# Issuing the attention stage's input loads from GpSimd's DMA ring instead of SyncE's

## The chip, the cores and the metric

The kernel runs on one core of a Trainium2 chip. The metric is the device time of one execution in microseconds (us). A core has five engines, each of which runs its own instruction stream in order: TensorE (PE, with its weight loads shown as PEld), VectorE (DVE), ScalarE (ACT), GpSimd (POOL) and SyncE (SP). They are kept in step by semaphores. Data moves between device memory and the on-chip memory by DMA: an engine issues a transfer, and the transfer tells of its landing through a semaphore.

## The reference

The program is a recurrent attention over 4 x 8 heads, 768 steps and 40 dimensions, followed by a two-layer MLP over 3072 tokens.

```python
# attention, for each of 32 heads; state is 40 x 40
for t in range(S):
    y[:, :, t] = np.einsum('bhd,bhde->bhe', rt, state)
    Sa = np.einsum('bhde,bhe->bhd', state, at)
    state_decay = state * wt[:, :, None, :] - np.einsum('bhd,bhe->bhde', Sa, bt)
    state = state_decay + np.einsum('bhd,bhe->bhde', vt, kt)
# MLP, d_model 320, d_ff 2048
h = x @ w_in
sp = np.maximum(h, 0.0) + np.log1p(np.exp(-np.abs(h)))
out = (h * erf(sp)) @ w_out
```

`r, k, v, w, a, b` come in float32; the MLP's weights come in float64 and are turned into float32 on the chip.

## The kernel before

The 768 steps are cut into blocks of 128 (`L`) and these into chunks of 32 (`C`). The 32 heads are worked on in two groups of 16 (`NG` = 2, eight pairs each), one after the other, so there are 12 stages of four chunks, 48 chunks in all. Within a chunk the recurrence becomes matrix products: `prep` makes running products of the decay `w` for a block, `aphase` scales `k`, `b` and `a` with them and builds the chunk's small matrices, `tphase` inverts a block's triangular matrices, and `chain` carries the state through the chunk. `load_x`, `mm1`, `unit` and `post` are the MLP for tokens whose attention is done; it runs beside the attention of later stages.

The order is not left to the engines. Every operation is entered with `Plan.add` (name, engine, function, what it reads and writes), and `Plan.schedule` then returns an order written out by hand in the file: `ORDER` is a list of operation numbers, `ENGINES` a string with one letter for each operation (P for PE, A for ACT, V for DVE, G for POOL, S for SP). With these two of the right length, no planner runs. -1 and lower in `ORDER` are filler matmuls (`warm`, L579). Each engine gets its operations in this order, and waits where a buffer or an input isn't ready.

All 907 DMAs of the kernel are entered through one helper, `dma`, and issued by SP (L576 in the profile, whatever the transfer). Those of the attention are:

- the input loads: `w` (12, 420 KB each, into `Pr`, in `prep`), `kba` (48, 416 KB, into `bk`; three of the first stage go into other tiles that are free then), `zv` (48, 80 KB, into `Zm`), `vx` (96, 40 KB, into `Vu`), `rt` (48, 104 KB, into `Rt`), `rv` (48, 416 KB, into `vt`);
- transfers of results, on which the attention's own chain runs: `zs` (`Zs<-Ab`), `AD`, `Ti`, `Ap`, `TD`, `tb` (through device memory, to change the layout) and `zu` (`Vu<-Us`).

Besides these there are the MLP weights (`wd`), the attention's result (`xw`, `xd<-Pr`), its way back as the MLP's input (`xr`), and the output (`out`).

How many buffers a load has decides how early it can be issued: `Pr` has three, `bk`, `vt`, `Rt` and `Vu` two, `Zm` one. The previous content of a buffer is read last by: `bk` the products at L677 and the transposes at L695, `Zm` the products at L785 (Z), `Rt` and `Vu` the products at L841 and L845 (MY), `vt` the products at L830 (PQ).

POOL does 120 operations of its own in this order, above all 27 products `nd` (L1039) and 27 `l` (L1051) of the MLP's activation, 19 `bk` (L672) and 10 `ab` (L667) of the attention, and 20 `xl` (L990), the low part of the MLP's input. DVE does the other operations of these kinds. After `nd` comes DVE's `r` (L1040), after `l` DVE's `h` (L1052); `nd` has one buffer.

Of the kernel before, what the change touches and what calls it, by code (L numbers as in the profile page):

```python
# [200 lines left out]
)  # L201
ENGINES = (
    "SSSVVGVGVGAAAVVGAGVVVAASAVVVVSVSSVPVVSSPVSGSSVPVVSSPASVSSGPVVSSPASVSSVPVVSSPASSSSAAVVVVVVVVVVVVVVVVVVVVVVVVVVVVSSSSVPPPPVPPPPVSVVAAAGAGSVVAA"
    "AVAVSVVAAAGAVSVVAAAVAVSVVAAAVAVSVVAAAVAVSVVAAAVAVSVVAAAGAVSVVAAAGAAVAGSVVAAAGAAVAGSVVAAAVSVVAAAVSVVAAAGSVVAAAVSVVAAAGSVVAAAVSVVAAAVSVVAAAVSV"
    "VAAAGSVVAAAVSAVVAVSVSSVPVVSSPASVSSVPVVSSPVSVSSVPVVSSPASVSSGPVVSSPASSSSSAAPAPAAVAVPVPVPVPVVSSSSSAAPVPAAAVVPAPAPVPVVSSSSSAAPAPAAAAAPAPVPVPVVSS"
    "SSSAAPAPAAAAVPVPVPVPVVSSSSSSSSAAVVVVVVVVVVVVVVVVVVVVVVVVVVVVSSSSVPPPPVPPPPVSAGSVGSSVVPPVAPPVAPPAAPPVAAAAAAAAAAAAAAAVVVVVVVVAAAAAPPAAPPAAVVPP"
    "PPPPAAGVPPPPPPAAVVPPPPVVPPPPSAVVAVSVSSGPVVSSPASGSSGPVVSSPASVSSGPVVSSPASVSSGPVVSSPASSSSSVVAPAPASSSSPVPAPVPVVSSSSSAAPAPASSSSPVPVPVPVVSSSSSVVPV"
    "PASSSSPAPVPVPVVSSSSSAAPAPASSSSPAPAPVPVVSSSSSSSSAAVVVVVVVVVVVVVVVVVVVVVVVVVVVVSSSSVPPPPVPPPPVSVGSVVSSAVAAAAAAAAAAAAAAVVGVVVGVAAAAAPPAAPPAAVVP"
    "PPPPPAAVVPPPPPPAAGVPPPPVVPPPPASASAAAAAAAAAAAAAAGVVVGVVVAAAAAPPAAPPVAGVPPPPPPAAVVPPPPPPAAVVPPPPGVPPPPSAVVVVSVSSVPVVSSPASGSSVPVVSSPASVSSVPVVSS"
    "PASVSSVPVVSSPASSSSSVAAPVPASSSSPVPVPVPVVSSSSSAAPAPASSSSPAPAPVPVVSSSSSAAPAPASSSSPAPAPVPVVSSSSSAVPVPVSSSSPVPAPVPVVSSSSSSSSAAVVVVVVVVVVVVVVVVVVV"  # L210
    "VVVVVVVVVSSSSVPPPPVPPPPVSVGSVVSSAGAAAAAAAAAAAAAAVVGVVVVVAAAAAPPAAPPAAGVPPPPPPAAVVPPPPPPAAVVPPPPVVPPPPASASAAAAAAAAAAAAAAGVVVVVVVAAAAAPPAAPPAA"
    "VVPPPPPPAAVVPPPPPPAAVVPPPPVVPPPPSAVVVVSVSSVPVVSSPVSGSSVPVVSSPASVSSVPVVSSPASVSSVPVVSSPASSSSSVAAPVPVSSSSPAPAPVPVVSSSSSVVPAPASSSSPAPAPVPVVSSSSS"
    "VAPAPASSSSPAPAPVPVVSSSSSAAPAPASSSSPAPAPVPVVSSSSSSSSAAVVVVVVVVVVVVVVVVVVVVVVVVVVVVSSSSVPPPPVPPPPVSVGSAVSSAVAAAAAAAAAAAAAAVVGVVVVVAAAAAPPAAPPA"
    "AGVPPPPPPAAVVPPPPPPAAVVPPPPVVPPPPASASAAAAAAAAAAAAAAVVGVVVVVAAAAAPPAAPPAAVVPPPPPPVAVVPPPPPPAAGVPPPPVVPPPPSAVVAVSVSSVPVVSSPASVSSGPVVSSPASVSSVP"
    "VVSSPASVSSGPVVSSPASSSSSVAAPAPASSSSPAPVPVPVVSSSSSAVPAPVSSSSPVPVPVPVVSSSSSAAPAPASSSSPAPAPVPVVSSSSSAVPAPVSSSSPVPAPVPVVSSSSSSSSAAVVVVVVVVVVVVVVV"
    "VVVVVVVVVVVVVSSSSVPPPPVPPPPVSAGSAGSSVGAAAAAAAAAAAAAAVVGVVVGVAAAAAPPAAPPAAVVPPPPPPAAGVPPPPPPAAVVPPPPVVPPPPASASAAAAAAAAAAAAAAVVVVVVVVAAAAAPPAA"
    "PPAAVVPPPPPPAAVVPPPPPPAAVVPPPPVVPPPPSAVVVVSVSSGPVVSSPVSGSSGPVVSSPASVSSVPVVSSPASVSSGPVVSSPASSSSSVAAPAPVSSSSPVPVPVPVVSSSSSVAPAPVSSSSPAPAPVPVVS"
    "SSSSVAPAPASSSSPAPAPVPVVSSSSSAAPAPASSSSPAPVPVPVVSSSSSSSSAAVVVVVVVVVVVVVVVVVVVVVVVVVVVVSSSSVPPPPVPPPPVSAGSAGSSVVAAAAAAAAAAAAAAVVGVVVVVAAAAAPPA"
    "APPAAVVPPPPPPAAGVPPPPPPAAVVPPPPVVPPPPASASAAAAAAAAAAAAAAGVVVVVVVAAAAAPPVAPPAAVVPPPPPPVAVVPPPPPPAAVVPPPPVVPPPPSAVVVVSVSSGPVVSSPASGSSGPVVSSPVSV"
    "SSGPVVSSPASVSSVPVVSSPASSSSSVVAPVPVSSSSPVPAPVPVVSSSSSAAPAPASSSSPVPAPVPVVSSSSSVAPAPASSSSPAPAPVPVVSSSSSAVPAPASSSSPAPAPVPVVSSSSSSSSAAVVVVVVVVVVV"  # L220
    "VVVVVVVVVVVVVVVVVSSSSVPPPPVPPPPVSAGSVVSSVVAAAAAAAAAAAAAAVVVVVVVVAAAAAPPAAPPAAGVPPPPPPAAGVPPPPPPAAVVPPPPGVPPPPASASAAAAAAAAAAAAAAVVVVVVVVAAAAA"
    "PPAAPPAAGVPPPPPPAAGVPPPPPPVAGVPPPPGVPPPPSAVVAVSVSSVPVVSSPVSVSSGPVVSSPASVSSVPVVSSPASVSSVPVVSSPVSSSSSVAAPVPASSSSPAPVPVPVVSSSSSAAPAPASSSSPVPAPV"
    "PVVSSSSSAAPAPASSSSPAPAPVPVVSSSSSVAPAPASSSSPAPVPVPVVSSSSSSSSAAVVVVVVVVVVVVVVVVVVVVVVVVVVVVSSSSVPPPPVPPPPVSVVSAGSSAVAAAAAAAAAAAAAAGVGVVVVVAAAA"
    "APPAAPPAAVVPPPPPPAAVVPPPPPPAAVVPPPPGVPPPPASASAAAAAAAAAAAAAAVVGVGVVVAAAAAPPVAPPVAGVPPPPPPAAVVPPPPPPAAGVPPPPGVPPPPSAVVAVSVSSVPVVSSPASGSSGPVVSS"
    "PASVSSVPVVSSPVSGSSVPVVSSPASSSSSVAAPVPVSSSSPAPAPVPVVSSSSSAVPVPASSSSPVPVPVPVVSSSSSAAPAPASSSSPAPAPVPVVSSSSSAAPAPASSSSPAPAPVPVVSSSSSSSSAAVVVVVVV"
    "VVVVVVVVVVVVVVVVVVVVVSSSSVPPPPVPPPPVSVGSAVSSVVAAAAAAAAAAAAAAGVVVVVVVAAAAAPPVAPPAAVVPPPPPPAAVVPPPPPPAAVVPPPPVVPPPPVSASAAAAAAAAAAAAAAVVGVVVGVA"
    "AAAAPPVAPPAAVVPPPPPPAAVVPPPPPPAAGVPPPPVVPPPPSAVVVVSVSSVPVVSSPASVSSVPVVSSPASVSSVPVVSSPVSGSSVPVVSSPASSSSSVVAPAPVSSSSPAPAPVPVVSSSSSAVPVPASSSSPV"
    "PVPVPVVSSSSSAAPAPASSSSPAPAPVPVVSSSSSAAPAPASSSSPAPAPVPVVSSSSSSSSAAVVVVVVVVVVVVVVVVVVVVVVVVVVVVSSSSVPPPPVPPPPVSAGSVGSSVGAAAAAAAAAAAAAAGVGVVVGV"
    "AAAAAPPAAPPAAVVPPPPPPAAVVPPPPPPAAVVPPPPVVPPPPASASAAAAAAAAAAAAAAVVGVVVVVAAAAAPPAAPPAAVVPPPPPPAAVVPPPPPPVAGVPPPPGVPPPPSAVVAVSVSSVPVVSSPVSGSSGP"
    "VVSSPASVSSGPVVSSPASVSSGPVVSSPASSSSSGAVPAPVSSSSPVPAPVPVVSSSSSAAPAPASSSSPVPAPVPVVSSSSSAAPAPASSSSPVPAPVPVVSSSSSAAPAPASSSSPVPVPVPVVSSSSSSSSAAVVV"  # L230
    "VVVVVVVVVVVVVVVVVVVVVVVVVSSSSVPPPPVPPPPVSAVSAGSSAGAAAAAAAAAAAAAAVVVVVVGVAAAAAPPVAPPAAGVPPPPPPVAVVPPPPPPVAVVPPPPGVPPPPASASAAAAAAAAAAAAAAGVGVG"
    "VVVAAAAAPPVAPPAAVVPPPPPPAAVVPPPPPPAAVVPPPPGVPPPPSSSSSVAVPVPASSSSPVPAPVPVVSSSSSVVPAPVSSSSPAPAPVPVVSSSSSAVPAPASSSSPVPVPVPVVSSSSSVVPVPASSSSPVPA"
    "PVPVVSSSSVPVVSVVSVVSSVGAAAAAAAAAAAAAAVVVVVVVVAAAAAPPAAPPAAVVPPPPPPVAVVPPPPPPAAVVPPPPVVPPPPVSASAAAAAAAAAAAAAAVVVVVVVVAAAAAPPVAPPAAVVPPPPPPAAV"
    "VPPPPPPVAVVPPPPGVPPPPAAAAAAAAAAAAAAVVVVVVVVAAAAAVVPPPPVVPPPPVVPPPPVVPPPPASAS"
)
# [259 lines left out]
class Net:  # L495
# [77 lines left out]
            self.eng(e).tensor_copy(o, i)  # L573

    def dma(self, name, o, i, rd=(), wr=(), pr=0):
        self.P.add(name, "SP", lambda e: self.nc.sync.dma_start(o(), i()), rd, wr, pr, ISSUE.get(name, 0.41))  # L576
# [618 lines left out]
```

## Time and profile before

| | |
|---|---|
| median of 3 runs | 859.44 us (858.28 to 864.45) |
| the profiled execution | 857.22 us, its span 855.2 us |
| granted TensorE clock, mean | 0.97 |
| DMA | 185585 packets, 107.58 MB, mean 126 GB/s |
| POOL | 17% busy, 124 instructions |

The profiled execution is 0.26% under the median of the three runs. The time of a kernel lies some 2 us above its span. A row of the profile names the line, the engine, the operation and the tiles it writes and reads (`out<-in`); all DMA issues have line L576, the helper's, so they are told apart by their tiles. `SPq` is SP's queue. Idle time is given with what ended it: `<-DMA x` is a transfer that landed, `<-PE y` an operation that finished.

### The profile page before, as it was taken

The numbers are of one execution on the slowest core, as the hardware profiler recorded it, in microseconds if no ns is written. First come the engines' busy times: TensorE is split into PE (matmuls) and PEld (weight loads), VectorE is DVE, ScalarE is ACT, GpSimd is POOL, SyncE is SP. The second block draws the span as 40 slices with busy tenths as digits, with TensorE's granted clock in tenths as the row PEclk, the third lists the DMA queues.
The fourth block names the chain that finished last, engine by engine and source line by source line (L and its number), as shares of the span: only waits on it lengthen the run. The fifth ranks groups of instructions, "written<-read, shape, count | busy, mean of one in ns | idle before, by whom it ended". The sixth has DMA issues, their size and how long they took to land.

```text
span 855.2 us, 32264 instructions
## 1 busy us (share of the span) xinstructions
PE 741.9 (87%) x13794; PEld 572.6 (67%) x13794; DVE 626.0 (73%) x1331; ACT 563.6 (66%) x1055; POOL 145.3 (17%) x124
## 2 busy tenths in 40 slices
...
GB/s 213 216 155 156 172 157 119 134 135 142 135 169 115 145 139 123 138 121 143 160 122 118 139 130 115 158 109 146 141 112 128 126 112 92 123 39 66 36 16 19
DMA packets 185585, 107.58 MB, mean 126 GB/s; under 512 B 134268, under 2 KB 167804, under 8 KB 185436
## 3 DMA queue, kind: packets, MB, share of 16 engines
q1 hardware_dynamic: 185436, 105.46, 51.8%
...
q14 instruction: 39, 0.32, 0.1%
...
## 4 chain that ended last, share of the span: by engine, by line
PE 43%; DMA 21%; DVE 14%; SPq 8%; ACT 6%; issue 6%; POOL 1%; DVEq 0%; ACTq 0%; POOLq 0%
PE po L1061 15%; PE ph L1006 10%; SPq L576 8%; DMA Zs<-Ab 3%; PE pA L740 3%; DMA Ti<-AD 3%; PE ph L579 3%; DMA Tb<-TD 2%; PE my L841 2%; PE pQ L830 2%; PE pA L677 2%; DMA bk<-in_kba_e 2%; DMA AD<-Zs 2%; DVE h L1052 2%; PE my L794 2%
## 5 line engine op out<-in xcount | busy, mean ns | idle before, releaser
L1061 PE MATMUL po<-wo,h 128*128 128x320 f32 x768 | 255.1, 459 | 6.1 <-DVE h L1052 5.8
L1061 PEld LDWEIGHTS po<-wo,h 128*128 128x128 f32 x768 | 135.7, 195 | 51.4 <-DVE h L1052 8.7
L1014 ACT ACTIVATE l<-l 128x512 f32<-128x512 f32 x192 | 112.0, 625 | 18.2 <-DVE nd L1039 14.4
L1006 PE MATMUL ph<-xh,wih 128*128 128x256 f32 x384 | 96.1, 332 | 3.4 <-ACT h L571 3.4
L1006 PE MATMUL ph<-xh,wil 128*128 128x256 f32 x384 | 78.0, 285 | 0.0
L1006 PE MATMUL ph<-xl,wih 128*128 128x256 f32 x384 | 77.7, 284 | 0.0
L1052 DVE SCALAR_TENSOR_TENSOR h<-l,h 128x512 f32<-128x512 f32 x96 | 70.3, 739 | 3.0 <-POOL l L1051 2.1
L1040 DVE SCALAR_TENSOR_TENSOR r<-nd,r 128x512 f32<-128x512 f32 x96 | 68.1, 709 | 5.9 <-POOL nd L1039 4.8
L1039 POOL TENSOR_TENSOR nd<-l,r 128x512 f32<-128x512 f32 x27 | 35.7, 1321 | 206.9 <-DVE r L1040 120.4
L1006 PEld LDWEIGHTS ph<-xh,wih 128*128 128x128 f32 x384 | 61.3, 194 | 10.2 <-ACT h L571 4.3
L571 ACT COPY Zm<-MT 40x320 f32<-40x320 f32 x71 | 32.4, 457 | 50.5 <-DVE MT L848 45.6
L579 PE MATMUL ph<-d 104*128 104x512 bf16 x257 | 65.7, 407 | 0.0
L1051 POOL TENSOR_TENSOR l<-l,r 128x512 f32<-128x512 f32 x27 | 38.2, 1419 | 158.6 <-ACT l L1014 85.8
L1006 PEld LDWEIGHTS ph<-xh,wil 128*128 128x128 f32 x384 | 60.6, 194 | 3.9 <-issue 3.9
L1014 ACT ACTIVATE l<-h 128x512 f32<-128x512 f32 x96 | 57.2, 628 | 7.2 <-DVE h L573 6.0
L1006 PEld LDWEIGHTS ph<-xl,wih 128*128 128x128 f32 x384 | 60.2, 192 | 0.0
L1039 DVE TENSOR_TENSOR nd<-l,r 128x512 f32<-128x512 f32 x69 | 49.7, 721 | 11.6 <-ACT r L1014 9.5
L1006 PE MATMUL ph<-xl,wir 128*128 128x256 f32 x192 | 54.9, 286 | 3.8 <-issue 3.7
L841 PE MATMUL my<-Vu,sg 64*40 64x72 f32 x1536 | 48.5, 233 | 8.7 <-DVE h L1052 3.1
L1014 ACT ACTIVATE r<-r 128x512 f32<-128x512 f32 x96 | 55.2, 624 | 0.4
L1014 ACT ACTIVATE r<-l 128x512 f32<-128x512 f32 x96 | 54.2, 619 | 1.5 <-DVE l L1051 1.4
L1006 PE MATMUL ph<-xh,wir 128*128 128x256 f32 x192 | 54.8, 285 | 0.0
...
## 6 DMA issues: line engine op xcount, KB each, us to landing
vt<-in_rv_e SPq DMA_DIRECT2D x48, 416.0 KB
bk<-in_kba_e SPq DMA_DIRECT2D x45, 416.0 KB
...
```

The costliest lines, as they stand in the source:

```text
L571: self.nc.scalar.copy(o, i)
L576: self.P.add(name, "SP", lambda e: self.nc.sync.dma_start(o(), i()), rd, wr, pr, ISSUE.get(name, 0.41))
L579: self.nc.tensor.matmul((self.ph[1], self.pQ)[x], self.d1[:, :128], self.d1[:, :512], start=True, stop=True)
L740: nc.tensor.matmul(pw[js, i], l[js, i], r[js, i], start=True, stop=True)
L841: nc.tensor.matmul(my[h * 64:h * 64 + 40, x, j], sg[xs, j, h], vu[xs, j // 2 * 2 + h, j % 2], start=True, stop=False)
L1006: nc.tensor.matmul(ph[:, j * 256:j * 256 + 256], a[:k, fs], b[:k], start=(m == 0), stop=(m == 7))
L1014: self.P.add(name, "ACT", lambda e: nc.scalar.activation(out=o, in_=i, **kw), rd, wr + ["act"], pr, 0.62)
L1039: P.add("nd", [("DVE", 0.69), ("POOL", 1.28)], lambda e, r=r, l=l, nd=nd: s.eng(e).tensor_tensor(out=nd, in0=l, in1=r, op=ALU.mult), [("l" ...
L1040: P.add("rho", "DVE", lambda e, r=r, nd=nd: nc.vector.scalar_tensor_tensor(out=r, in0=nd, scalar=2 * C4, in1=r, op0=ALU.add, op1=ALU.mult) ...
L1051: P.add("E", [("POOL", 1.28), ("DVE", 0.69)], lambda e: s.eng(e).tensor_tensor(out=l, in0=l, in1=r, op=ALU.mult), [("r", ir)], [("l", il)] ...
L1052: P.add("G", "DVE", lambda e: nc.vector.scalar_tensor_tensor(out=h, in0=l, scalar=-1.0, in1=h, op0=ALU.add, op1=ALU.mult), [("l", il)], [( ...
L1061: nc.tensor.matmul(po, h[:, bs], s.wo[:, f], start=(f == 0), stop=(f == 15))
```

## The change

Six names of loads are put in a tuple `BULK`. `dma` enters a load of these names for POOL and issues it there; every other DMA stays with SP. In `ENGINES` the 300 letters of these loads turn from S to G, so that the list fits. `ORDER` is untouched: the loads keep their places among all operations, and so come into POOL's stream between the products that stand around them in `ORDER`, while SP's stream has 607 DMAs instead of 907.

```diff
@@ -200,36 +200,36 @@
 ENGINES = (
-    "SSSVVGVGVGAAAVVGAGVVVAASAVVVVSVSSVPVVSSPVSGSSVPVVSSPASVSSGPVVSSPASVSSVPVVSSPASSSSAAVVVVVVVVVVVVVVVVVVVVVVVVVVVVSSSSVPPPPVPPPPVSVVAAAGAGSVVAA"
...
+    "SSSVVGVGVGAAAVVGAGVVVAAGAVVVVGVSSVPVVSSPVGGSSVPVVSSPAGVSSGPVVSSPAGVSSVPVVSSPASSSSAAVVVVVVVVVVVVVVVVVVVVVVVVVVVVSSSSVPPPPVPPPPVSVVAAAGAGSVVAA"
...
@@ -253,6 +253,7 @@
 FREE = ("Am", "PQm", "MT", "Ym", "zt", "zmu", "us", "vtu", "ysM", "bTc", "ob", "hc", "Wm", "Tb", "zgb", "zcb")
+BULK = ("kba", "rt", "zv", "rv", "vx", "w")
...
@@ -573,7 +574,7 @@
     def dma(self, name, o, i, rd=(), wr=(), pr=0):
-        self.P.add(name, "SP", lambda e: self.nc.sync.dma_start(o(), i()), rd, wr, pr, ISSUE.get(name, 0.41))
+        self.P.add(name, "POOL" if name in BULK else "SP", lambda e: self.eng(e).dma_start(o(), i()), rd, wr, pr, ISSUE.get(name, 0.41))
```

`self.eng(e)` is `nc.gpsimd` for POOL and `nc.sync` for SP.

More of the change, by code (lines that the diff above doesn't have):

```diff
@@ L202 @@
 ENGINES = (
-    "SSSVVGVGVGAAAVVGAGVVVAASAVVVVSVSSVPVVSSPVSGSSVPVVSSPASVSSGPVVSSPASVSSVPVVSSPASSSSAAVVVVVVVVVVVVVVVVVVVVVVVVVVVVSSSSVPPPPVPPPPVSVVAAAGAGSVVAA"
+    "SSSVVGVGVGAAAVVGAGVVVAAGAVVVVGVSSVPVVSSPVGGSSVPVVSSPAGVSSGPVVSSPAGVSSVPVVSSPASSSSAAVVVVVVVVVVVVVVVVVVVVVVVVVVVVSSSSVPPPPVPPPPVSVVAAAGAGSVVAA"
     "AVAVSVVAAAGAVSVVAAAVAVSVVAAAVAVSVVAAAVAVSVVAAAVAVSVVAAAGAVSVVAAAGAAVAGSVVAAAGAAVAGSVVAAAVSVVAAAVSVVAAAGSVVAAAVSVVAAAGSVVAAAVSVVAAAVSVVAAAVSV"
-    "VAAAGSVVAAAVSAVVAVSVSSVPVVSSPASVSSVPVVSSPVSVSSVPVVSSPASVSSGPVVSSPASSSSSAAPAPAAVAVPVPVPVPVVSSSSSAAPVPAAAVVPAPAPVPVVSSSSSAAPAPAAAAAPAPVPVPVVSS"
@@ L206 @@
[L206 to L209, printed above, removed]
@@ L210 @@
-    "PASVSSVPVVSSPASSSSSVAAPVPASSSSPVPVPVPVVSSSSSAAPAPASSSSPAPAPVPVVSSSSSAAPAPASSSSPAPAPVPVVSSSSSAVPVPVSSSSPVPAPVPVVSSSSSSSSAAVVVVVVVVVVVVVVVVVVV"
+    "VAAAGSVVAAAVGAVVAVGVSSVPVVSSPAGVSSVPVVSSPVGVSSVPVVSSPAGVSSGPVVSSPAGGGGGAAPAPAAVAVPVPVPVPVVGGGGGAAPVPAAAVVPAPAPVPVVGGGGGAAPAPAAAAAPAPVPVPVVGG"
+    "GGGAAPAPAAAAVPVPVPVPVVSSSSSSSSAAVVVVVVVVVVVVVVVVVVVVVVVVVVVVSSSSVPPPPVPPPPVSAGSVGSSVVPPVAPPVAPPAAPPVAAAAAAAAAAAAAAAVVVVVVVVAAAAAPPAAPPAAVVPP"
+    "PPPPAAGVPPPPPPAAVVPPPPVVPPPPGAVVAVGVSSGPVVSSPAGGSSGPVVSSPAGVSSGPVVSSPAGVSSGPVVSSPAGGGGGVVAPAPASSSSPVPAPVPVVGGGGGAAPAPASSSSPVPVPVPVVGGGGGVVPV"
@@ L211 @@
+    "PASSSSPAPVPVPVVGGGGGAAPAPASSSSPAPAPVPVVSSSSSSSSAAVVVVVVVVVVVVVVVVVVVVVVVVVVVVSSSSVPPPPVPPPPVSVGSVVSSAVAAAAAAAAAAAAAAVVGVVVGVAAAAAPPAAPPAAVVP"
+    "PPPPPAAVVPPPPPPAAGVPPPPVVPPPPASASAAAAAAAAAAAAAAGVVVGVVVAAAAAPPAAPPVAGVPPPPPPAAVVPPPPPPAAVVPPPPGVPPPPGAVVVVGVSSVPVVSSPAGGSSVPVVSSPAGVSSVPVVSS"
+    "PAGVSSVPVVSSPAGGGGGVAAPVPASSSSPVPVPVPVVGGGGGAAPAPASSSSPAPAPVPVVGGGGGAAPAPASSSSPAPAPVPVVGGGGGAVPVPVSSSSPVPAPVPVVSSSSSSSSAAVVVVVVVVVVVVVVVVVVV"
     "VVVVVVVVVSSSSVPPPPVPPPPVSVGSVVSSAGAAAAAAAAAAAAAAVVGVVVVVAAAAAPPAAPPAAGVPPPPPPAAVVPPPPPPAAVVPPPPVVPPPPASASAAAAAAAAAAAAAAGVVVVVVVAAAAAPPAAPPAA"
-    "VVPPPPPPAAVVPPPPPPAAVVPPPPVVPPPPSAVVVVSVSSVPVVSSPVSGSSVPVVSSPASVSSVPVVSSPASVSSVPVVSSPASSSSSVAAPVPVSSSSPAPAPVPVVSSSSSVVPAPASSSSPAPAPVPVVSSSSS"
@@ L213 @@
-    "VAPAPASSSSPAPAPVPVVSSSSSAAPAPASSSSPAPAPVPVVSSSSSSSSAAVVVVVVVVVVVVVVVVVVVVVVVVVVVVSSSSVPPPPVPPPPVSVGSAVSSAVAAAAAAAAAAAAAAVVGVVVVVAAAAAPPAAPPA"
-    "AGVPPPPPPAAVVPPPPPPAAVVPPPPVVPPPPASASAAAAAAAAAAAAAAVVGVVVVVAAAAAPPAAPPAAVVPPPPPPVAVVPPPPPPAAGVPPPPVVPPPPSAVVAVSVSSVPVVSSPASVSSGPVVSSPASVSSVP"
-    "VVSSPASVSSGPVVSSPASSSSSVAAPAPASSSSPAPVPVPVVSSSSSAVPAPVSSSSPVPVPVPVVSSSSSAAPAPASSSSPAPAPVPVVSSSSSAVPAPVSSSSPVPAPVPVVSSSSSSSSAAVVVVVVVVVVVVVVV"
+    "VVPPPPPPAAVVPPPPPPAAVVPPPPVVPPPPGAVVVVGVSSVPVVSSPVGGSSVPVVSSPAGVSSVPVVSSPAGVSSVPVVSSPAGGGGGVAAPVPVSSSSPAPAPVPVVGGGGGVVPAPASSSSPAPAPVPVVGGGGG"
@@ L216 @@
+    "VAPAPASSSSPAPAPVPVVGGGGGAAPAPASSSSPAPAPVPVVSSSSSSSSAAVVVVVVVVVVVVVVVVVVVVVVVVVVVVSSSSVPPPPVPPPPVSVGSAVSSAVAAAAAAAAAAAAAAVVGVVVVVAAAAAPPAAPPA"
+    "AGVPPPPPPAAVVPPPPPPAAVVPPPPVVPPPPASASAAAAAAAAAAAAAAVVGVVVVVAAAAAPPAAPPAAVVPPPPPPVAVVPPPPPPAAGVPPPPVVPPPPGAVVAVGVSSVPVVSSPAGVSSGPVVSSPAGVSSVP"
+    "VVSSPAGVSSGPVVSSPAGGGGGVAAPAPASSSSPAPVPVPVVGGGGGAVPAPVSSSSPVPVPVPVVGGGGGAAPAPASSSSPAPAPVPVVGGGGGAVPAPVSSSSPVPAPVPVVSSSSSSSSAAVVVVVVVVVVVVVVV"
     "VVVVVVVVVVVVVSSSSVPPPPVPPPPVSAGSAGSSVGAAAAAAAAAAAAAAVVGVVVGVAAAAAPPAAPPAAVVPPPPPPAAGVPPPPPPAAVVPPPPVVPPPPASASAAAAAAAAAAAAAAVVVVVVVVAAAAAPPAA"
-    "PPAAVVPPPPPPAAVVPPPPPPAAVVPPPPVVPPPPSAVVVVSVSSGPVVSSPVSGSSGPVVSSPASVSSVPVVSSPASVSSGPVVSSPASSSSSVAAPAPVSSSSPVPVPVPVVSSSSSVAPAPVSSSSPAPAPVPVVS"
@@ L218 @@
-    "SSSSVAPAPASSSSPAPAPVPVVSSSSSAAPAPASSSSPAPVPVPVVSSSSSSSSAAVVVVVVVVVVVVVVVVVVVVVVVVVVVVSSSSVPPPPVPPPPVSAGSAGSSVVAAAAAAAAAAAAAAVVGVVVVVAAAAAPPA"
-    "APPAAVVPPPPPPAAGVPPPPPPAAVVPPPPVVPPPPASASAAAAAAAAAAAAAAGVVVVVVVAAAAAPPVAPPAAVVPPPPPPVAVVPPPPPPAAVVPPPPVVPPPPSAVVVVSVSSGPVVSSPASGSSGPVVSSPVSV"
-    "SSGPVVSSPASVSSVPVVSSPASSSSSVVAPVPVSSSSPVPAPVPVVSSSSSAAPAPASSSSPVPAPVPVVSSSSSVAPAPASSSSPAPAPVPVVSSSSSAVPAPASSSSPAPAPVPVVSSSSSSSSAAVVVVVVVVVVV"
+    "PPAAVVPPPPPPAAVVPPPPPPAAVVPPPPVVPPPPGAVVVVGVSSGPVVSSPVGGSSGPVVSSPAGVSSVPVVSSPAGVSSGPVVSSPAGGGGGVAAPAPVSSSSPVPVPVPVVGGGGGVAPAPVSSSSPAPAPVPVVG"
```

21 lines of the change are left out of this document (12 added, 9 removed).

## The prediction

> **What bounds the kernel now.** I read the page first (engine shares, DMA queues, the chain that ended last), then stretches of the span, then who waits on SP and on POOL. From the page:
>
> ```profile
> span 855.2 us, 32264 instructions
> PE 741.9 (87%) x13794; PEld 572.6 (67%) x13794; DVE 626.0 (73%) x1331; ACT 563.6 (66%) x1055; POOL 145.3 (17%) x124
> ...
> q1 hardware_dynamic: 185436, 105.46, 51.8%
> ...
> PE 43%; DMA 21%; DVE 14%; SPq 8%; ACT 6%; issue 6%; POOL 1%; DVEq 0%; ACTq 0%; POOLq 0%
> ```
>
> No engine is full. PE carries 43% of the chain, but transfers (21%) and SP's issuing (8%, 0.08 x 855 = 68 us) stand there too, and POOL hardly does. All of the kernel's own DMAs use one queue, q1. Three stretches (start, middle, tail; columns: PE, PEld, DVE, ACT and POOL busy, clock, DMA share, GB/s) say where there is room:
>
> ```profile
> 0.00:130.00 130.00, 87.13 (x1258) 47.73 (x1258) 91.65 (x194) 56.39 (x115) 20.74 (x23) 0.97 0.69 178
> 130.00:760.00 630.00, 568.58 (x11758) 457.94 (x11759) 476.82 (x1034) 437.99 (x825) 111.62 (x92) 0.97 0.56 129
> 760.00:855.00 95.00, 86.21 (x780) 66.97 (x779) 57.52 (x103) 69.27 (x115) 12.94 (x9) 0.96 0.14 37
> ```
>
> In the 630 us of the middle PE is idle for 61 us: that is about all that better feeding can win there. The granted clock is 0.96 to 0.97 in all three, so I expect nothing from it. The moved loads fall into the first two stretches.
>
> **The change part by part.** Six kinds of load leave SP's queue: kba, rt, zv, rv (48 each), vx (96) and w (12), 300 DMAs. Their cost on SP (durations in ns: min/median/max; then the first and last start):
>
> ```profile
> L576 SPq DMA_DIRECT2D Vu<-in_v_x x96: 564/612/4873, 6.0 to 767.0; - x96
> ...
> L576 SPq DMA_DIRECT2D Rt<-in_r_e x48: 308/410/2245, 2.1 to 769.4; - x48
> L576 SPq DMA_DIRECT2D Zm<-in_v_s x48: 315/426/1214, 23.1 to 768.7; - x48
> L576 SPq DMA_DIRECT2D vt<-in_rv_e x48: 307/480/2112, 30.6 to 768.2; - x48
> ...
> L576 SPq DMA_DIRECT2D bk<-in_kba_e x45: 310/395/1407, 7.7 to 691.3; - x45
> ...
> L576 SPq DMA_DIRECT2D Pr<-in_w_e x12: 333/502/1499, 2.6 to 610.0; - x12
> ```
>
> At the medians: vx 96 x 0.612 = 59 us, rt 20, zv 20, rv 23, kba 48 x 0.395 = 19 (three of the 48 go into other tiles), w 6: **147 us leave SP**, 0.49 us each.
>
> *Gain 1, SP's issuing.* The 300 are a third of SP's 907 issues (the counts of that view, added up); a third of the chain's 68 us would be 22 us at most, if nothing else is late next.
>
> *Gain 2, SP's waits.* Much of the order on SP is held by loads whose data no DMA on SP reads:
>
> ```profile
> SPq L576 <- PE my L845: 12.4, 7, 3.3
> ...
> SPq L576 <- PE my L785: 10.6, 4, 8.3
> ...
> SPq L576 <- DMA Pr<-in_w_e: 6.1, 5, 1.9
> ...
> SPq L576 <- DMA vt<-in_rv_e: 4.5, 6, 1.6
> ```
>
> The first two (23 us, 11 waits) are mostly loads that wait for their buffer: zv has one, read by Z at L785; rt and vx are read at L845. [...] Behind them stand the transfers of the chain (Zs<-Ab, AD<-Zs, Vu<-Us). About 33 us of waits leave SP; as SP is 8% of the chain, most cover one another with other work. I take 5 us.
>
> *Gain 3, one ring less shared.* The same small transfer takes very different times on the chain:
>
> ```profile
> 502.05 2.80 DMA Zs<-Ab
> 508.40 5.79 DMA Zs<-Ab
> ```
>
> And this is the size of the two large kinds of load:
>
> ```profile
> vt<-in_rv_e SPq DMA_DIRECT2D x48, 416.0 KB
> bk<-in_kba_e SPq DMA_DIRECT2D x45, 416.0 KB
> ```
>
> With 48 of each that is 2 x 48 x 416 KB = 40,000 KB, 41 MB of q1's 105. If the 3.0 us between the two Zs<-Ab is time behind such loads, a second ring gives some of it back. The DMA part of the chain is 0.21 x 855 = 180 us; at most half of it could shrink so (2.80 of 5.79). The lower bound is 0: the engines that move the bytes stay the same and are 56% busy in the middle. I take 8 us, near zero because the total work of those engines doesn't change. A rule that weighs on this term is in the Trainium skill, "DMA: Bandwidth & Descriptors", section "Issuing engines are not separate DMA queues": transfers from all issuers run on the same 16 engines and interleave, and only issue time is saved. By it this term is 0 and the sum below 8 us worse; the trace of before has one ring and can't show it.
>
> Of gains 1 to 3 (22 + 5 + 8 = 35 us) PE's program order lets through what its idle time can hold; next late are DVE's results (14% of the chain). I count 20 us.
>
> *Loss 1, POOL's own queue.* POOL executes in order, and each load now stands between its products. The rows (busy, mean ns, idle before):
>
> ```profile
> L1051 POOL TENSOR_TENSOR l<-l,r 128x512 f32<-128x512 f32 x27 | 38.2, 1419 | 158.6 <-ACT l L1014 85.8 <-DVE r L1040 64.0 <-ACT Us L571 7.5
> L1039 POOL TENSOR_TENSOR nd<-l,r 128x512 f32<-128x512 f32 x27 | 35.7, 1321 | 206.9 <-DVE r L1040 120.4 <-ACT r L1014 86.5
> L672 POOL TENSOR_TENSOR bk<-bk,Wt 104x512 f32<-104x512 f32 x18 | 24.5, 1362 | 57.3 <-DMA bk<-in_kba_e 46.9 <-PE pQ L821 4.0 <-PE pA L695 3.3
> L990 POOL TENSOR_TENSOR xl<-xr,xh 128x256 fp32r<-128x256 f32 (+1 forms) x20 | 15.8, 797 | 124.6 <-ACT xh L571 62.2 <-DVE xh L573 56.9 <-DMA vt<-in_rv_e 5.5
> L667 POOL TENSOR_TENSOR Ab<-bk,Pr 104x512 f32<-104x512 f32 x9 | 10.9, 1208 | 39.4 <-PE pA L677 21.5 <-DMA AD<-Zs 10.4 <-DVE vt L573 7.5
> L1039 DVE TENSOR_TENSOR nd<-l,r 128x512 f32<-128x512 f32 x69 | 49.7, 721 | 11.6 <-ACT r L1014 9.5
> L1040 DVE SCALAR_TENSOR_TENSOR r<-nd,r 128x512 f32<-128x512 f32 x96 | 68.1, 709 | 5.9 <-POOL nd L1039 4.8
> ```
>
> The trace shows no DMA issued by POOL. Lower bound: SP's own 0.49 us. Upper bound: a full product on POOL, 1.42 us (L1051). The nearest row is the same product on both engines: POOL needs 1321/721 = 1.83 times DVE's time; 0.49 x 1.83 = **0.90 us** each, my estimate. 300 x 0.90 = 270 us, POOL 145 + 270 = 415 us, 49% of the span; it stays below the others' busy time, so it hurts through lateness alone. 101 products stand in those five rows, with 300/101 = 3 loads between two of them. In 270/855 = 0.32 of the time a load is being issued; a product that comes then waits for half of three loads, 1.35 us: 0.43 us on average, 43 us over 101 products. To this come the buffer waits that moved along from SP (23 us, now ahead of products instead of DMAs); with a product due every 855/101 = 8.5 us and two waits in three well inside a gap I count 10. Who waits: DVE's r (L1040) behind nd. One such place, POOL's and then DVE's row:
>
> ```profile
> 331.53 1.29 POOL L1039 TENSOR_TENSOR nd<-l,r 128x512 f32<-128x512 f32 x1 [4.86 <-DVE r L1040]
> 332.95 0.68 DVE L1040 SCALAR_TENSOR_TENSOR r<-nd,r 128x512 f32<-128x512 f32 x1
> ```
>
> nd ends at 332.82 and r starts 0.13 us later: no slack, and the DVE queue behind r stands still with it. POOL's xl and bk feed PE with more room. I let 60% of 53 us reach the end: 32 us.
>
> *Loss 2, the loads' arrival.* kba is issued just in time: POOL waits 46.9 us in 9 waits for it to land (the bk row above), DVE in
>
> ```profile
> DVE bk L672 <- DMA bk<-in_kba_e: 8.2, 5, 3.8
> PE my L785 <- DMA Zm<-in_v_s: 4.6, 5, 1.5
> ```
>
> If POOL needs 0.5 us more to issue, these 19 waits grow by up to 10 us, and a zv or kba that stands behind a product waiting for DVE (120.4 us of such idle in the nd row) comes later still. Against that, loads no longer queue behind SP's other 607 issues. I take 3 us. The rest (same instructions, order and bytes) costs nothing; rt, rv and vx have two buffers, and only single waits for them show.
>
> **Sum.** -20 + 32 + 3 = +15 us. Against the profiled execution (857.2 us with its span of 855.2) that is 872; that execution is 2.2 us under the median of the three runs, 859.4, so against the median **874 us**.
>
> **The rivals.**
> *A second ring wins (faster).* If POOL issues in about SP's 0.49 us, loads take 147/855 = 0.17 of its time, a product waits 0.17 x 0.74 = 0.13 us, 13 us in all, perhaps 8 at the end. With gain 3 at 25 us instead of 8 the gains are 22 + 5 + 25 = 52; half of it passes: 859 - 26 + 8 = **841**. For it: the waits on SP and 5.79 against 2.80. Against: PE's 61 us of idle time is all there is in the middle. It decides where an issue costs under about 0.6 us. The Trainium skill, same page, "Queues, rings and completion order", says that an engine takes its rings in turn, packet by packet; that is the mechanism of this case, and no run here shows it yet.
> *No change.* Loads lead their use, SP's time was covered by others, and POOL's idle 83% covers the issues: **860**. The same comes out if the moved loads still show on q1, so that only issue time moves.
> *POOL nearly full (much slower).* At the upper bound, 1.42 us, loads take 426 us, POOL 571 (67%); the mean wait is 0.50 x 2.13 = 1.06 us, 107 us in all, 70 of them at the end; from about 2 us (145 + 600 = 745, PE's own 742) POOL is the bound: **925 and up**. For it: POOL is slower than DVE on like work. The Trainium skill, "SBUF — State Buffer", section "SBUF: two separate sides", says that POOL can't write its descriptors while DVE runs an operation that uses both ports; the trace of before can't show it.
>
> **How the numbers follow.** My case (POOL's lateness beats SP's relief) 0.36, POOL nearly full 0.10, no change 0.22, faster 0.32. Measurement of this kernel tells about 1% from no change; by that bound: faster 0.32, same 0.22, slower 0.46. The range takes in the faster case and the lower end of the worst, and leaves out some 0.07 below and 0.10 above: 836 to 930. My case's own range is 864 to 902 (the same sum with 0.7 and 1.3 us an issue).
>
> **What would show it.** A second queue in the queue section with 41 MB and more; SP's moved rows gone, its waits for in_w_e and in_rv_e gone; chain share of SPq at 5 to 6%; POOL busy near 49%, its DMA rows at 0.7 to 1.3 us; DVE r and h waiting for POOL 30 us or more, against 4.8 for r now; Zs<-Ab nearer 3 us on the chain if gain 3 is real. Wrong if POOL's issues come out near 0.5 us, or if DVE's waits for POOL don't grow.

## The result

| | kernel before | changed kernel |
|---|---|---|
| median | 861.95 us of 4 runs (858.28 to 865.93) | 900.85 us of 4 runs (896.91 to 905.01) |
| ratio | 1 | 1.045 [1.037, 1.053] |
| span of the profiled execution | 855.2 us | 896.3 us |
| granted TensorE clock in it | 0.970 | 0.955 |

The changed kernel is 4.5% slower, some 39 us. (The ratios here and below leave disturbed runs out, the medians do not, so a ratio can differ a little from the quotient of the medians.) These are the answering lines of its page: the span, busy time and share of each engine, and the two DMA queues (packets, MB, share of 16 engines' span).

```profile
span 896.3 us, 32401 instructions
...
PE 756.7 (84%) x13794; PEld 584.3 (65%) x13794; DVE 633.0 (71%) x1331; ACT 563.9 (63%) x1055; POOL 312.3 (35%) x424
...
q0 software_dynamic: 20736, 59.05, 23.7%
q1 hardware_dynamic: 138768, 46.42, 22.3%
```

The move itself is there: a second queue carries 59 of the 105 MB, and POOL has 300 instructions more. POOL is busy for 312 us, 35%, so no engine has become full. PE does the same 13794 matmuls in 756.7 us instead of 741.9, and stands still for 896.3 - 756.7 = 139.6 us instead of 855.2 - 741.9 = 113.3. Of the 41.1 us that the span grew, 26.3 are idle time of PE and 14.8 are longer matmuls; 741.9 x 0.970 / 0.955 = 753.6 would be their time by the lower clock alone.

The same three stretches as before (PE, PEld, DVE, ACT, POOL busy, clock, DMA share, GB/s) say where; the last 41 us of the changed kernel lie behind them:

```profile
0.00:130.00 130.00, 90.71 (x1393) 49.99 (x1394) 94.72 (x203) 58.37 (x119) 42.39 (x62) 0.97 0.66 184
130.00:760.00 630.00, 549.78 (x10992) 443.92 (x10990) 458.77 (x991) 414.80 (x783) 241.27 (x329) 0.95 0.49 123
760.00:855.00 95.00, 85.04 (x1276) 68.22 (x1277) 57.07 (x101) 64.98 (x113) 27.37 (x32) 0.95 0.23 59
```

At the start the changed kernel is ahead: PE does 90.7 us of work in the first 130 us, against 87.1. In the middle it falls behind, 549.8 against 568.6 us of work in the same 630 us, and what is left over runs in the tail (DMA share 0.23 against 0.14).

What POOL does now (busy, mean ns, idle time before the group and what ended it):

```profile
L577 POOL DMA_DIRECT2D Vu<-in_v_x x96 | 58.3, 609 | 40.6 <-PE my L846 34.5 <-PE my L786 3.6 <-issue 2.4
L1052 POOL TENSOR_TENSOR l<-l,r 128x512 f32<-128x512 f32 x27 | 39.1, 1448 | 72.1 <-ACT l L1015 55.5 <-DVE r L1041 16.6
L1040 POOL TENSOR_TENSOR nd<-l,r 128x512 f32<-128x512 f32 x27 | 35.5, 1314 | 86.8 <-DVE r L1041 58.8 <-ACT r L1015 25.4 <-issue 2.5
L577 POOL DMA_DIRECT2D Rt<-in_r_e x48 | 27.5, 574 | 48.1 <-PE my L846 48.1
L577 POOL DMA_DIRECT2D vt<-in_rv_e x48 | 27.2, 567 | 50.0 <-PE pQ L831 26.9 <-ACT Ti L719 6.6 <-ACT h L572 5.6
L577 POOL DMA_DIRECT2D bk<-in_kba_e x45 | 25.7, 572 | 58.0 <-PE pA L696 26.2 <-issue 18.1 <-PE pQ L822 13.3
L577 POOL DMA_DIRECT2D Zm<-in_v_s x48 | 25.6, 533 | 36.7 <-PE my L786 36.7
...
L577 POOL DMA_DIRECT2D Pr<-in_w_e x12 | 6.8, 568 | 19.1 <-DVE zt L574 5.3 <-DVE l L938 4.7 <-DVE nd L1040 4.6
```

Two things are to be seen. An issue takes POOL 0.53 to 0.61 us, whether it moves 40 KB or 420 KB. And POOL stands still in front of these loads for 40.6 + 48.1 + 50.0 + 58.0 + 36.7 + 19.1 = 252.5 us, mostly until PE has read the buffer that the load is to fill (PE ended 189.3 us of it by these rows). The idle time in front of `nd` and `l` has fallen (from 207 and 159 us to 87 and 72): part of the time in which POOL used to wait for a product's input, it now waits for a load's buffer. If the product's input comes meanwhile, nobody takes it.

One such place, first POOL's timeline (start, duration, idle before it and what ended it), then DVE's:

```profile
199.44 0.58 POOL L577 DMA_DIRECT2D bk<-in_kba_e  x1 [2.02 <-PE pA L696]
203.02 0.55 POOL L577 DMA_DIRECT2D bk<-in_kba_e  x1 [3.00 <-issue]
203.59 1.30 POOL L1040 TENSOR_TENSOR nd<-l,r 128x512 f32<-128x512 f32 x1
```

```profile
199.49 0.69 DVE L1041 SCALAR_TENSOR_TENSOR r<-nd,r 128x512 f32<-128x512 f32 x1
...
204.92 0.69 DVE L1041 SCALAR_TENSOR_TENSOR r<-nd,r 128x512 f32<-128x512 f32 x1 [3.04 <-POOL nd L1040]
205.71 0.69 DVE L1040 TENSOR_TENSOR nd<-l,r 128x512 f32<-128x512 f32 x1
206.32 0.48 DVE L849 TENSOR_TENSOR MT<-MT,my 104x320 f32<-104x320 f32 x1
```

POOL waits 3.00 us (for this one the profile names nothing that ended the wait), issues the load of `bk`, and starts `nd` 0.02 us after it; `nd` takes 1.30 us and DVE's `r` follows at once, after 3.04 us of nothing. Two places behind `r` in DVE's queue stands `MT`, a step of the attention's own chain. Over the whole span (waiting engine and operation, released by; us in all, times, longest), first the kernel before, then the changed one:

```profile
ACT Ti L718 <- DMA Ti<-AD: 15.1, 7, 3.6
...
DVE T L733 <- DMA Tb<-TD: 14.3, 10, 3.2
...
DVE Ab L667 <- DMA Zs<-Ab: 11.7, 13, 2.5
...
DVE h L1052 <- POOL l L1051: 2.1, 2, 1.2
```

```profile
DVE r L1041 <- POOL nd L1040: 18.4, 8, 3.5
...
ACT Ti L719 <- DMA Ti<-AD: 16.9, 7, 4.0
...
DVE T L734 <- DMA Tb<-TD: 14.7, 10, 3.4
...
ACT l L1015 <- POOL nd L1040: 10.6, 5, 4.1
...
DVE bk L673 <- DMA bk<-in_kba_e: 6.8, 5, 2.1
...
PE my L786 <- DMA Zm<-in_v_s: 6.1, 2, 4.1
...
DVE Ab L668 <- DMA Zs<-Ab: 5.1, 6, 1.8
...
DVE h L1053 <- POOL l L1052: 5.0, 3, 2.9
```

Waits for POOL's products grew from 4.8 (`r`) and 2.1 (`h`) to 18.4 + 10.6 + 5.0 = 34 us. The products themselves didn't become slower: `nd` takes 1314 ns on POOL after 1321, `l` 1448 after 1419. The waits for three of the transfers on the attention's chain, which now share SP's ring with less, sum to 36.7 us after 41.1: not much won (`Zs<-Ab` alone fell from 11.7 to 5.1 us, the other two grew). And SP, with 300 DMAs fewer, waits for those who make what it is to move:

```profile
SPq L576 <- DVE Zs L684: 12.5, 18, 1.8
```

```profile
SPq L577 <- DVE Zs L685: 55.6, 27, 6.5
```

It reaches its DMAs earlier and then stands there: these transfers were not waiting for SP alone.

### The profile page after: what moved, and what is told of

The parts are those of the page before. It is cut to its first block, busy times and chain, and to the rows that moved or that the text cites. A ratio compares the mean times of both kernels' runs of the same rounds, so it can differ in the third digit from the quotient of the medians.

```text
span 896.3 us, 32401 instructions
## 1 busy us (share of the span) xinstructions
PE 756.7 (84%) x13794; PEld 584.3 (65%) x13794; DVE 633.0 (71%) x1331; ACT 563.9 (63%) x1055; POOL 312.3 (35%) x424
## 3 DMA queue, kind: packets, MB, share of 16 engines
q0 software_dynamic: 20736, 59.05, 23.7%
q1 hardware_dynamic: 138768, 46.42, 22.3%
## 5 line engine op out<-in xcount | busy, mean ns | idle before, releaser
L1062 PE MATMUL po<-wo,h 128*128 128x320 f32 x768 | 258.5, 464 | 6.8 <-DVE h L1053 6.8
L1041 DVE SCALAR_TENSOR_TENSOR r<-nd,r 128x512 f32<-128x512 f32 x96 | 69.8, 727 | 19.7 <-POOL nd L1040 18.4
L577 POOL DMA_DIRECT2D Vu<-in_v_x x96 | 58.3, 609 | 40.6 <-PE my L846 34.5
L1040 POOL TENSOR_TENSOR nd<-l,r 128x512 f32<-128x512 f32 x27 | 35.5, 1314 | 86.8 <-DVE r L1041 58.8
L1052 POOL TENSOR_TENSOR l<-l,r 128x512 f32<-128x512 f32 x27 | 39.1, 1448 | 72.1 <-ACT l L1015 55.5
L842 PE MATMUL my<-Vu,sg 64*40 64x72 f32 x1536 | 50.4, 238 | 12.5 <-issue 4.3
L685 DVE TENSOR_TENSOR Zs<-pA,tri 64x256 f32<-64x256 f32 x96 | 40.6, 423 | 26.0 <-PE pA L678 24.2
```

The lines of the kernel that those rows point to most:

```text
L577: self.P.add(name, "POOL" if name in BULK else "SP", lambda e: self.eng(e).dma_start(o(), i()), rd, wr, pr, ISSUE.get(name, 0.41))
L685: P.add("Am", "DVE", lambda e, x=x, xs=xs: nc.vector.tensor_tensor(out=zx[64:128, x], in0=pz[xs], in1=s.tri[xs, None, :].to_broadcast([64, ...
L842: nc.tensor.matmul(my[h * 64:h * 64 + 40, x, j], sg[xs, j, h], vu[xs, j // 2 * 2 + h, j % 2], start=True, stop=False)
L1040: P.add("nd", [("DVE", 0.69), ("POOL", 1.28)], lambda e, r=r, l=l, nd=nd: s.eng(e).tensor_tensor(out=nd, in0=l, in1=r, op=ALU.mult), [("l" ...
L1041: P.add("rho", "DVE", lambda e, r=r, nd=nd: nc.vector.scalar_tensor_tensor(out=r, in0=nd, scalar=2 * C4, in1=r, op0=ALU.add, op1=ALU.mult) ...
L1052: P.add("E", [("POOL", 1.28), ("DVE", 0.69)], lambda e: s.eng(e).tensor_tensor(out=l, in0=l, in1=r, op=ALU.mult), [("r", ir)], [("l", il)] ...
```

## The experiments

Four theories go into these runs. O: the time in which POOL is occupied with issuing delays its products. W: products come late because they stand behind loads that wait for a buffer. L: the loads are late in POOL's queue, whatever else POOL does. C, formed after the first four runs: loads and products hold each other up, in both directions, because one in-order queue holds both. All ratios are to the kernel before, run on the same chip, with 95% intervals.

**Occupancy alone.** The loads stay with SP. At the place of each of the 300, POOL fills a scratch tile twice and waits for nothing.

```diff
...
-        self.P.add(name, "SP", lambda e: self.nc.sync.dma_start(o(), i()), rd, wr, pr, ISSUE.get(name, 0.41))
+        def fn(e):
+            if name in BULK:
+                self.nc.gpsimd.memset(self.scr, 0.0)
+                self.nc.gpsimd.memset(self.scr, 0.0)
+            self.nc.sync.dma_start(o(), i())
...
+        self.P.add(name, "SP", fn, rd, wr, pr, ISSUE.get(name, 0.41))
```

> All loads stay on SP as before; at the place of each of the 300 loads POOL does two memsets of 128x224 (about 0.57 us together by the 0.31 us of the 128x256 memset row), which wait for nothing, and so is busy for about 170 us more. Theory O (the time that POOL spends on issuing makes its products late): most of the 39 us, 885 to 900 us. Theory W (products stand behind loads that wait for their buffers): 860 to 868 us, since nothing waits. Theory L (the loads themselves come later from POOL's ring): no change, 860 to 864 us.

Measured: 863.73 against 858.44 us, 1.004 [1.001, 1.008]. The page shows POOL as busy as in the changed kernel:

```profile
PE 748.7 (87%) x13794; PEld 575.7 (67%) x13794; DVE 629.1 (73%) x1331; ACT 563.6 (65%) x1055; POOL 311.0 (36%) x724
```

311.0 us of busy time, at the same places, costs 0.4% where the changed kernel's 312.3 us cost 4.5%, and DVE's `r` waits 7.0 us for `nd`, not 18.4. Theory O falls: it explains about 3 of the 39 us.

**Half of the loads.** Of the six names only three are given to POOL, the large ones (108 DMAs) or the small ones (192). (Here and in the runs on the first stages a second edit, left out below, makes an operation that has only one allowed engine take that one instead of its letter in `ENGINES`.)

```diff
-BULK = ("kba", "rt", "zv", "rv", "vx", "w")
+BULK = ('kba', 'rv', 'w')
...
```

> Only kba, rv and w are on POOL (108 loads, 45 of the 59 MB; in the changed kernel's profile some 55 to 75 us of POOL's waits before loads). Theory W: about a third of the loss, 870 to 880 us. Theory O: 108/300 of it, about 876 us. Theory L: four fifths of it by bytes, 890 us or more.

```diff
-BULK = ("kba", "rt", "zv", "rv", "vx", "w")
+BULK = ('rt', 'zv', 'vx')
...
```

> Only rt, zv and vx are on POOL (192 loads, 14 of the 59 MB; 119 us of POOL's waits before loads, by the rows of the changed kernel: 48.1 + 36.7 + 34.5). Theory W: the larger part of the loss, 880 to 892 us. Theory O: 192/300 of it, about 887 us. Theory L: under a quarter of it by bytes, 870 us or less.

Measured: 881.56 us, 1.028 [1.020, 1.036], and 876.61 us, 1.022 [1.014, 1.030]. Each half costs about half; 2.8 + 2.2 = 5.0% against 4.5% for both. It is not one kind of load, and the loss goes neither by bytes (45 of the 59 MB are in the large ones) nor by number (192 of the 300 are small ones). It does go by POOL's waits in front of the loads: in the rows of the changed kernel above these are 50.0 + 58.0 + 19.1 = 127.1 us for the large ones and 40.6 + 48.1 + 36.7 = 125.4 us for the small ones. The first expectation had counted only 55 to 75 us for the large ones, so its share for theory W was too low. By their times alone, just above W's range in the first run and between W's and L's in the second, the two runs decide nothing.

**Products ahead of loads.** In the changed kernel's order, 129 loads of POOL go behind POOL's next product, where their first reader stands at least 30 places behind that product and the product fewer than 120 places behind the load.

```diff
...
-        order = N.P.schedule()
+        order = N.P.products_first(N.P.schedule(), 30)
```

> All 300 loads on POOL, but 129 of them go behind the product that follows them on POOL (those whose first reader stands at least 30 places behind that product in the written order), so that fewer products stand behind a waiting load. Theory W: half of the loss or more goes, 865 to 882 us, and DVE's r waits less for POOL's nd than 18.4 us. Theory O: the issuing stays, 890 to 900 us. Theory L: loads come later still, 900 us or more.

Measured: 898.43 us, 1.050 [1.040, 1.059], no better than the changed kernel. Its loads and its waits, in its profiled execution, which at 888.65 us was the shortest of the four:

```profile
L605 POOL DMA_DIRECT2D Vu<-in_v_x x96 | 58.7, 613 | 12.0 <-PE my L874 7.5 <-PE my L814 3.6 <-issue 0.8
...
L605 POOL DMA_DIRECT2D Rt<-in_r_e x48 | 27.5, 573 | 4.8 <-PE my L874 4.8
L605 POOL DMA_DIRECT2D vt<-in_rv_e x48 | 27.5, 572 | 8.3 <-PE pQ L859 7.7 <-ACT l L1043 0.6
L605 POOL DMA_DIRECT2D Zm<-in_v_s x48 | 25.7, 535 | 52.1 <-PE my L814 52.1
L605 POOL DMA_DIRECT2D bk<-in_kba_e x45 | 25.5, 568 | 71.4 <-PE pA L724 31.7 <-PE pQ L850 14.1 <-issue 13.9
```

```profile
PE my L814 <- DMA Zm<-in_v_s: 9.6, 4, 5.0
DVE bk L701 <- DMA bk<-in_kba_e: 9.4, 4, 4.3
...
DVE r L1069 <- POOL nd L1068: 5.8, 4, 2.4
```

POOL waits much less in front of three kinds of load (12.0, 4.8 and 8.3 us, after 40.6, 48.1 and 50.0), but more in front of `Zm` (52.1 after 36.7) and `bk` (71.4 after 58.0); with 5.2 us for `Pr` it is 153.8 us in all, after 252.5. DVE's `r` waits for `nd` 5.8 us instead of 18.4, and with `h` (6.0) and ACT's `l` (2.2) the waits for POOL's products are 14 us instead of 34. So products come less late, and nothing is won: some loads now stand behind products that wait for DVE and ACT, and `Zm` and `bk` are waited for longer (9.6 after 6.1, 9.4 after 6.8). These two rows have grown by only 6 us, so where the rest of the gain went is not shown. Late products alone, as theory W has it, do not carry the loss. From this came theory C, and a test that takes one of the two sides off POOL altogether.

**The products off POOL.** POOL's 103 products (`nd`, `l`, `bk`, `ab`, `xl`) go to DVE, once with the loads on SP (the control) and once with the loads on POOL.

```diff
             for o, e in zip(ops, self.engines):
                 o["eng"] = dict(P="PE", A="ACT", V="DVE", G="POOL", S="SP")[e]
+                if o["name"] in ('nd', 'E', 'xl', 'bk', 'ab') and o["eng"] == "POOL":
+                    o["eng"] = "DVE"
```

(`E` is the operation that the profile shows as `l`.)

> The control: all loads on SP as before, and the 103 products that POOL did for the attention and the MLP (nd, l, xl, bk, ab) are on DVE, at the same places of the order; POOL is left with a few operations at the start. DVE gets 103 products of about 0.7 us, some 70 us more. All theories: 870 to 900 us, from DVE's time alone; what counts is the difference to the next run.

> As the changed kernel, all 300 loads on POOL, and the 103 products on DVE as in the control: nothing but loads is left in POOL's queue in the middle. Theory C (POOL's one queue ties loads and products together: each waits in order behind the other): the loss is gone, at most 0.5% above the control, or below it by the 7 us by which the changed kernel was ahead at 185 us. Theory L (loads from POOL's ring come later, or two rings hinder one another): still 3 to 4.5% above the control.

Measured: the control 854.47 us, 1.001 [0.995, 1.006]; with the loads on POOL 854.39 us, 1.002 [0.997, 1.006]. The control's own expectation was wrong: DVE, busy for 626 us before, took 103 products more (659.5 us) at no cost. It is busy for only 33.5 us more, about half of the 70 expected, because its other operations became shorter once POOL had no products. Its `h`, which was on DVE all along, is an example, before and in the control:

```profile
L1052 DVE SCALAR_TENSOR_TENSOR h<-l,h 128x512 f32<-128x512 f32 x96 | 70.3, 739 | 3.0 <-POOL l L1051 2.1
```

```profile
L1054 DVE SCALAR_TENSOR_TENSOR h<-l,h 128x512 f32<-128x512 f32 x96 | 65.1, 685 | 1.0
```

With this, the four combinations are:

| | products on POOL | products on DVE |
|---|---|---|
| loads on SP | 1 | 1.001 [0.995, 1.006] |
| loads on POOL | 1.045 [1.037, 1.053] | 1.002 [0.997, 1.006] |

Neither side costs anything alone; the loss is there only when both share POOL's queue. That is theory C; L falls, since the loads are in POOL's queue in both cells of the lower row. (The cells were measured on different chips, each against the kernel before on the same chip.) That both directions count, late products and late loads, is not shown by the table; it is argued from the run before. POOL's loads in the kernel of the lower right cell, and its engines:

```profile
L579 POOL DMA_DIRECT2D bk<-in_kba_e x45 | 25.4, 565 | 176.4 <-PE pA L698 93.9 <-PE pQ L824 59.8 <-DMA AD<-Zs 10.8
L579 POOL DMA_DIRECT2D Zm<-in_v_s x48 | 25.4, 529 | 117.0 <-PE my L788 116.8 <-issue 0.2
```

```profile
PE 743.3 (87%) x13794; PEld 574.6 (67%) x13794; DVE 662.2 (78%) x1434; ACT 564.7 (66%) x1055; POOL 187.8 (22%) x321
```

POOL waits even longer in front of a load (176.4 us before `bk`, 58.0 in the changed kernel), and it costs nothing: in the middle only other loads stand behind the load. The long wait in a queue is harmless or not by what is behind it.

**Half of the products off POOL.** The loads stay on POOL; either the MLP's 54 products go to DVE, or the attention's 49.

```diff
+                if o["name"] in ('nd', 'E') and o["eng"] == "POOL":
+                    o["eng"] = "DVE"
```

> The changed kernel with the MLP's 54 products nd and l on DVE instead of POOL; the attention's 49 products (bk, ab, xl) stay on POOL beside the 300 loads. If the coupling is between the two pieces of work that share POOL (the MLP's products, which wait for DVE and ACT, and the attention's loads, which wait for PE), it is gone here: 0.995 to 1.012 of the kernel before. If any product beside the loads costs alike, 49 of 103 products keep about half of the 4.5%: 1.017 to 1.028. POOL's rows: its loads then wait less behind DVE's r.

```diff
+                if o["name"] in ('xl', 'bk', 'ab') and o["eng"] == "POOL":
+                    o["eng"] = "DVE"
```

> The changed kernel with the attention's 49 products bk, ab and xl on DVE; the MLP's 54 products stay on POOL beside the 300 loads. If the coupling is between the MLP's products and the attention's loads: nearly the whole loss stays, 1.030 to 1.050. If any product beside the loads costs alike: 1.018 to 1.028. If the attention's own products carry it: 0.995 to 1.010.

Measured: 874.65 us, 1.026 [1.019, 1.033], and 878.61 us, 1.025 [1.014, 1.036]. Each set of products alone keeps about half of the loss, as the case "any product beside the loads costs alike" had it. The half is rough: the executions of the first kernel lie between 860.80 and 878.38 us. I had thought that the MLP's products carry it, because they follow another rhythm than the attention's loads; that is not so.

**The loads of the first stages.** The changed kernel was ahead at its start, so only the loads of the first two and of the first three of the twelve stages go to POOL (50 and 75 DMAs).

```diff
-        self.P.add(name, "POOL" if name in BULK else "SP", lambda e: self.eng(e).dma_start(o(), i()), rd, wr, pr, ISSUE.get(name, 0.41))
+        self.P.add(name, "POOL" if name in BULK and self.P.tag in ('_0', '_1') else "SP", lambda e: self.eng(e).dma_start(o(), i()), rd, wr, pr, ISSUE.get(name, 0.41))
...
```

> Only the loads of the first two stages (50 of the 300) are on POOL; from the third stage on SP issues them as before. In the changed kernel everything was some 7 us early until 185 us and late after that. Theory C: the gain of the start stays, and nothing is lost later: 850 to 856 us. Theory L: a sixth of the loss, 863 to 868 us.

> As the run before, with the third stage's loads too (75 of the 300). Theory C: products of the MLP begin within this stage, so it is like the run before or some us worse, 850 to 860 us. Theory L: a quarter of the loss, 865 to 872 us.

> The loads of the first six of the twelve stages on POOL, the products where they were. The start's gain of about 7 us comes in the first 185 us, the loss of the changed kernel from about 190 us on. If the loss runs evenly over the middle, the three further stages lose some 12 to 20 us of the gain: 1.003 to 1.015. If the first six stages lose nothing and the gain goes on: below 0.985.

Measured: two stages 850.40 us, 0.994 [0.990, 0.999], as theory C had it; three stages 845.27 us, 0.989 [0.982, 0.995], below all that was expected. The run meant for six stages tested something else: the code tags only the first three and the last two stages, so its operations and their order are those of the run before it. It is a second measurement of three stages, on another chip, 848.42 us, 0.993 [0.989, 0.998], and its expectation stays untested. All three intervals lie below 1: some 0.6 to 1.1% faster than the kernel before, a version that beats both, though by little. The transfers `Vu<-Us` of the attention's chain show when (duration min/median/max in ns, then first and last start); in turn the kernel before, the changed one, three stages, and all loads on POOL with the products on DVE:

```profile
L576 SPq DMA_DIRECT2D Vu<-Us x176: 585/605/1823, 141.2 to 784.4; - x176
```

```profile
L577 SPq DMA_DIRECT2D Vu<-Us x176: 585/622/1702, 134.3 to 824.5; - x176
```

```profile
L579 SPq DMA_DIRECT2D Vu<-Us x176: 585/607/1710, 136.5 to 776.3; - x176
```

```profile
L579 SPq DMA_DIRECT2D Vu<-Us x176: 585/615/1617, 133.9 to 779.8; - x176
```

The first starts come 4.7 to 7.3 us earlier in all three kernels that issue the first stages' loads from POOL. The changed kernel turns 6.9 us ahead into 40.1 us behind by the last; the other two stay ahead, by 8.1 and 4.6 us. (The control of the last one, with its loads on SP, has 138.8 to 783.5, so of the last one's lead of 7.3 and 4.6 us the loads' issuer accounts for 4.9 and 3.7.)

**Three stages, and the products off POOL.** Both edits together, with the tags of the first three stages and all 103 products on DVE.

> The loads of the first three stages on POOL, and all 103 products on DVE. If the gain of these three stages is the second queue's at the start, it stays or grows a little without products beside it: 0.980 to 0.992. If DVE, full in the first stages, misses POOL's help there: 0.995 to 1.005.

Measured: 850.77 us, 0.997 [0.992, 1.001]. It lies in the second of the two expected ranges, though its interval reaches into the first: nothing is won over three stages with the products left on POOL. Whether DVE misses POOL's help there, as that case had it, was not looked into.

## Why the prediction was right, and where not

The direction and the range held, and the mechanism in outline: the kernel is slower because POOL's in-order queue now holds loads and products, and SP's relief does not pay for it. What did not hold is the largest term of the loss, products that wait while POOL is issuing. The sum was +15 us and the measurement +39. That 900.85 us also lies in my case's own range of 864 to 902 us is luck: that range was worked out with 0.7 and 1.3 us an issue, and an issue takes 0.57. The terms stand like this.

*Gains 1 to 3, 20 of 35 us counted.* The two kernels with the products on DVE differ in the loads' issuer alone, and their medians are 854.47 and 854.39 us: all gains together, with the loads' arrival (loss 2), come to nothing there within about 0.7%, or 6 us, by these intervals. A gain was seen at the start only, 5 to 7 us, and it had not been told apart as a place of its own in the sum. Of gain 2's 33 us, the four rows of SP's waits added up, the two rows of waits for a load to land are gone from SP, though no run shows why it had waited there; over the whole span SP's freed time went into waits for producers (12.5 to 55.6 us for `Zs`).

*Gain 3, 8 us.* The waits for three chain transfers went from 41.1 to 36.7 us while the kernel got slower: a few us, and not seen in the kernel's time. The rule weighed there, of the Trainium skill, "DMA: Bandwidth & Descriptors", section "Issuing engines are not separate DMA queues", that another issuer saves issue time alone, would have made it 0, and the runs agree with it: 854.47 against 854.39 us.

*The price of an issue, 0.90 us.* It is 0.53 to 0.61 us, near the lower bound of 0.49. Scaling by what POOL needs for a product was the wrong neighbour: issuing 40 KB takes 0.61 us and issuing 416 KB 0.57, so it doesn't grow with the tile as a product does. POOL is therefore 35% busy and not 49%.

*Loss 1, 43 us of lateness by occupancy and 10 us by buffer waits.* These two were mis-sized, in opposite directions. Occupancy alone costs 0.4%, about 3 us, where 60% of 43, so 26 us, had been let through. The waits moved along with the loads were counted at 10 us, on the ground that a product was due only every 8.5 us; what is left of the loss, some 36 us, is there only where loads that wait and products share the queue. The 23 us read on SP before were the wrong measure of them: POOL stands still in front of these loads for 252.5 us. Probably SP, with 607 other DMAs in its order, came to them later; this was not looked into.

*Sum.* The loss was counted at 35 us and measured at about 39, the gains at 20 and measured at about 0. So the total missed by the gains, and the loss came out near its size through two errors that cancel, which is luck.

*The rivals.* "A second ring wins" was to decide below about 0.6 us an issue. An issue came out at 0.57, and the kernel was slower all the same: the price of an issue was not the point that decides. For the same reason the last sentence of the prediction was half wrong: issues near 0.5 us don't refute it, only waits for POOL that don't grow would have. Those grew, from 4.8 us (`r`) to 18.4, with `h` to 23.4 of the 30 foretold, and to 34 with ACT's `l`, which had not been named. "POOL nearly full" didn't come about: POOL is 35% busy, and with DVE 71% busy its issues stay at 0.53 to 0.61 us. "No change" is out by the interval, 1.037 to 1.053.

*What the page was to show.* The second queue is there with 59 MB, and the waits for `in_w_e` and `in_rv_e` on SP are gone from the list of its longest waits. The share of SPq in the chain can't be compared, because the chain in the changed kernel's page breaks off after about a fifth of the span. In the kernel with products ahead of loads, whose chain covers 99% of its span, SPq has 4% (8% in the kernel before, 5 to 6% foretold) and POOL 4% (1% before).

What stays open: which part of the loss goes through late products and which through late loads, since pushing the loads back shortened the waits for products and lengthened others; and why the first three stages gain on POOL with the products beside them, while the whole set loses. Which of the later stages lose was not measured.
